# Attention and feed-forward in one kernel: half-swapped q and k weights issued by ScalarE, a swapped copy of x next on SP's queue, one copy of an up product on VectorE

## The chip, the cores and the metric

The kernel runs on one core of a Trainium2 chip. The metric is the time of one execution on the device, in microseconds (us); it is taken several times, and the median is compared. The times of trace rows below come from one profiled execution, counted from its first instruction. The engines are TensorE (PE for matmuls, PEld for weight loads), VectorE (DVE), ScalarE (ACT), GpSimd (POOL) and SyncE (SP); an engine's name with a q behind it (SPq, ACTq) means its queue of issued DMAs.

## What is computed

A transformer block with attention and feed-forward side by side, on 2048 rows of 448 numbers, bfloat16:

```python
xn = layernorm(x)
return x + A(xn, wqkv, wo) + B(xn, w_gate, w_up, w_down)

# A: 16 heads of 28, a row sees itself and the 255 rows before it
q, k, v = split(xn @ wqkv)
p = softmax(where(0 <= i - j < 256, q @ k.T * 28 ** -0.5, -1e9))
A = (p @ v) @ wo
# B: the hidden size is 1792
B = (gelu(xn @ w_gate) * (xn @ w_up)) @ w_down
```

## The kernel before

The 2048 rows are worked in four blocks of 512 (`qb`), the rows of a block in four tiles of 128. The contraction length 448 is three chunks of 128 and a remainder of 64, or seven chunks of 64. The code makes use of the seven chunks: a matmul over 64 rows takes half of TensorE's array, and two such matmuls, one on the upper and one on the lower 64 partitions, run side by side for two different products ("a pair"). For that, each half needs every chunk of normalised, transposed x (`xnT`) on its own 64 partitions. `xsw` is the copy of `xnT` with the two halves of partitions exchanged, and `swap` (L377) makes it by DMA, from SBUF to SBUF, in two pieces, one for each half. The weights for q and k get the same treatment: `wsq` holds half of `wqp` and half of `wkp`, exchanged, and `swap_weights` (L385) makes it by two DMAs of 192 KB. The pair for value tiles (`v_pair`, matmuls at L319) reads `xnT`, `xsw`, `wv`, `wvs`; the pair for q and k of four heads (`qk_pair`, L333) reads `xnT`, `xsw`, `wqp`, `wkp`, `wsq`.

The order of work is written out by hand: each engine works through its instructions in the order of the program. A block consists of attention in nine or ten steps (`steps_of`, `attention`) and then the gates of the feed-forward (`gated`). A step is: scores on TensorE (L600) into a PSUM tile of which attention has one buffer (`score_pool(1)`), an exp on ScalarE over all of it (L604), masks (on GpSimd in the first block, L528), and then work that fills TensorE, taken from `plan`. Products of attention weights with values (`pv`, L570) come two steps or more later. Generators hand out filling work in small pieces, and an entry like `(u, 11)` in `plan` takes eleven of them.

In the first block the filling work is, in this order: `gen_qk`, which finishes q and k of the block's own rows; `gen_up` with the pairs p = 1, 2, 3, 0 of the up product (matmuls at L401, two PSUM tiles each); and from the sixth step on `gen_pairs(1, ...)`, which makes values, q and k for the second block: the value pair of tiles 4 and 5, the value pair of tiles 6 and 7, then q and k. The up products are copied from PSUM to `hT` (L418); the second copy of a pair goes to ScalarE if p is in `shared`, else to VectorE. Four PSUM tiles, handed out in the order in which they come free (`take`, `give`), serve all of these.

`ahead3` (L720), called in the third step of the first block, normalises tiles 5, 6, 7 of x on VectorE, transposes each by a DMA on SP's queue (L175), and issues on SP's queue: the swap of tiles 4 and 5, `swap_weights`, the swap of tiles 6 and 7, and then the loads of gate weights, x, up weights, output weights and down weights. `fill_pads(False)` puts pad columns into `wqp` and `wkp` on GpSimd (L283, L285). SP issues in this order, and each issue waits for what its transfer reads. Copies on the hardware queues take their completion semaphores in turn out of eight, so an issue may also wait for the transfer that had the same semaphore before.

Of the kernel before, what the change touches and what calls it, by code (L numbers as in the profile page):

```python
# [17 lines left out]
P = 128  # L18
# [8 lines left out]
def kernel(  # L27
# [11 lines left out]
    nc = tc.nc  # L39
# [98 lines left out]
    wsq = const.tile([P, 3, H, 32], bf16, name="wsq")  # L138
# [13 lines left out]
    def stat(t):  # L152
        st = work.tile([P, nc.vector.BN_STATS_DIM], f32, name="st")
        nc.vector.bn_stats(out=st[:, :], in_=x_sb[:, t, :])  # L154
        nc.vector.bn_aggr(out=mv_all[:, t, :], in_=st[:, :])
# [44 lines left out]
    spare = ["b0", "b1", "b2", "b3"]  # L200
# [37 lines left out]
    def ring(qb):  # L238

        return slice(qb % 2 * QB, (qb % 2 + 1) * QB)  # L240
# [18 lines left out]
    def gen_qk(gs, others):  # L259

        for g in gs:
            pq = take("pq")
            proj(pq, wqp, 0, g)
            yield 650
            pk = take("pk")
            proj(pk, wkp, 0, g)
            yield 650
            if g in others:
                v_half(*others[g])
            qk_halves(0, g, pq, pk)  # L270
            if g in others:
                v_copy(*others[g], nc.vector.tensor_copy)
            qk_copies(0, g, pq, pk)
            yield 360

    def fill_pads(last):


        def put(dst, src, n, lo):

            src = src.rearrange("p (j d) -> p j d", d=Dh)[:, :, lo:]
            if n == 4:
                nc.gpsimd.tensor_copy(out=dst[:, 12:16, Dh:32], in_=src[:, :, 24:28])  # L283
            src = src[:, :, 0:24].rearrange("p j (g i) -> p g j i", i=8)[:, :, :, 0:4]
            nc.gpsimd.tensor_copy(out=dst[:, 0:12, Dh:32].rearrange("p (g j) i -> p g j i", j=4), in_=src)  # L285

        if not last:
            for c in range(3):
                k = wraw[:, c, D + 12 * Dh:2 * D]
                put(wqp[:, c, :, :], k, 4, 0)  # L290
                put(wkp[:, c, :, :], k, 3, 4)
            return
        put(w3p[0:64, :, :], w3k[0:64, :], 4, 0)
        put(w3p[64:128, :, :], w3k[64:128, :], 3, 4)
        nc.gpsimd.memset(w3p[64:128, 12:16, :], 0.0)
# [81 lines left out]
    def swap(qb, t=None, n=4):  # L377

        t0 = P * (4 * qb if t is None else t)
        to = t0 - qb * QB + ring(qb).start  # L380
        for hi in range(2):
            nc.sync.dma_start(out=xsw[64 * hi:64 * hi + 64, :, to:to + n * P],
                              in_=xnT[64 - 64 * hi:P - 64 * hi, 0:3, t0:t0 + n * P])

    def swap_weights():  # L385

        for hi, src in enumerate((wqp, wkp)):
            nc.sync.dma_start(out=wsq[64 * hi:64 * hi + 64], in_=src[64 - 64 * hi:P - 64 * hi, 0:3])

    def xchunk(qb, hi, c, t0, n):  # L390

# [280 lines left out]
    pvs = [take("pv", D)]  # L672
# [47 lines left out]
    def ahead3():  # L720
        for t in (5, 6, 7):
            norm(t)
            dma_transp(t)
        swap(1, 4, 2)
        fill_pads(False)
        swap_weights()
        swap(1, 6, 2)
        load_ffn(wg, B_w_gate, slice(0, 3))
        nc.sync.dma_start(out=x_sb[:, 12:16, :], in_=xv[:, 12:16, :])
        load_ffn(wu, B_w_up, slice(4, 7))  # L730
        load_ffn(wg, B_w_gate, slice(3, 7))
        wo_v = A_wo.rearrange("(g j d) n -> j d g n", g=4, j=4)
        for j in range(4):
            nc.sync.dma_start(out=wo[32 * j:32 * j + Dh, :, :], in_=wo_v[j])
        for k in (0, 7):
            nc.sync.dma_start(out=wd[:, k:k + 7, :], in_=rows(B_w_down, k, 7))

    for qb in range(NB):
        if qb in (1, 3):
            tc.mark_branch_hint_location("general", hint="LikelyTaken",  # L740
                                         engines=[mybir.EngineType.DVE if qb == 1 else mybir.EngineType.PE])
        early = ()
        if qb == 0:
            new_hT(0)
            early = (0, 1, 2, 3)
            u = chain(gen_qk((1, 2, 3), {1: (3, pvs[3]), 2: (2, pvs[2])}), gen_up(0, (1, 2, 3, 0), (2, 3)))
            w = gen_pairs(1, (("v", 0), ("v", 2), ("k", 0), ("k", 1), ("k", 2)))
            plan = [[(u, 2), ahead, (u, 1)], [lambda: v_dense(2, pvs[2]), (u, 2), ahead2, (u, 1)],
                    [lambda: spare.append(spare.pop(1)), (u, 2), ahead3, (u, 4)], [lambda: stat(8), (u, 11)],
                    [lambda: stat(9), (u, 7), lambda: stat(10), (u, 7), lambda: fill_pads(True)], [(w, 7), "sums", "inverse"],  # L750
                    [(w, 11)], [lambda: stat(11), (w, 6), lambda: rstd(8, 4)],
                    [lambda: q_last(1, nc.vector.tensor_copy), (w, 4), "sums", "inverse", (w, 7)]]
        else:
            d = gen_down(qb - 1)
            if qb < 3:
                u = gen_pairs(qb + 1, (("v", 0), ("k", 0), ("v", 2), ("k", 1), ("k", 2)))
                plan = [[(d, 14)], [(d, 11)], [(d, 11)], [(u, 7)], [(d, 18)], ["sums", (u, 7), "inverse"], [(u, 12)],
                        [(u, 9)], [lambda: q_last(qb + 1, nc.vector.tensor_copy), (d, 5), "sums", "inverse"], [(d, 13)]]
                if qb == 1:
                    for i in range(4):  # L760
                        plan[i].insert(0, lambda t=12 + i: stat(t))
                    plan[4].append(lambda: rstd(12, 4))
            else:
                new_hT(3)
                early = (1, 2, 3, 4, 5, 6)
                u = gen_up(3, early)
                plan = [[(d, 14)], [(d, 4), (u, 5)], [(u, 9)], [(u, 7)], [(d, 18)], [(u, 7)], [(d, 13)], [(d, 5), (u, 7)],
                        [(u, 7)], [(d, 18)]]
        if qb in (1, 2):
            swap(qb + 1)  # L770
        score_pool(1)
        rest, after, flush = attention(qb, plan)
        nc.scalar.preload_act_table(ACT.Gelu_apprx_tanh)
        score_pool(2)
        if qb not in hTs:
            new_hT(qb)

        def hook(f):
            after(f)
            if qb < 3 and f == 4:  # L780
                collect(qb + 1)
            if qb < 3 and f == 10:
                deliver(qb + 1)
            t = ({0: 8, 4: 9, 8: 10, 10: 11} if qb == 0 else {4: 12, 6: 13, 8: 14, 10: 15} if qb == 1 else {}).get(f)
            if t is not None:
                norm(t)
                dma_transp(t)

        gated(qb, early, rest, flush, hook)
        if qb < NB - 1:  # L790
            nc.scalar.preload_act_table_set("natural_log_exp_and_others")
# [151 lines left out]
```

## Time and profile before

| | us |
|---|---|
| median of 3 executions | 216.72 |
| the three executions | 218.1, 216.69, 216.72 |
| the profiled execution | 218.75 |
| its span, first to last instruction | 216.9 |
| busy: TensorE, VectorE, ScalarE, GpSimd | 209.9, 159.3, 131.5, 46.9 |
| TensorE busy, first 56 us | 52.7 |
| TensorE busy, the 160.9 us behind | 157.2 |

The granted clock of TensorE is 1.00 in every stretch of the profile. A line of the timeline begins with start and duration in us, then engine, source line, operation, tile written and tiles read, the size, and the number of instructions merged into the line. In brackets stands the idle time of the engine before it and what ended it. Several merged lines of TensorE overlap, because matmuls on the two halves of the array do. A row of the chain of waits has start, duration and what; a row of the view of waits has the waiting engine and line, what it waited for, and total us, times and longest wait.

### The profile page before, as it was taken

The page shows a single profiled execution, that of the slowest core. Times are in us where ns is not written, and L with a number is a line of the kernel's source. Part 1 is how long each engine was busy: PE and PEld are TensorE (multiplying, and loading weights), DVE is VectorE, ACT ScalarE, POOL GpSimd, SP SyncE. Part 2 cuts the span into 40 slices and gives each one's busy share as a digit, 9 for nine tenths or more (in the row PEclk, how much of TensorE's full clock was granted, in tenths as well). Part 3 has the DMA queues.
Part 4 walks back from the last instruction along what each step waited for, and adds up shares of the span by engine and source line. Part 5 has one row for each costly group of instructions (what it writes and reads, how often), then busy time and mean ns, then how long its engine had stood idle before and what let it go on. Part 6 is the DMA issues. An engine that isn't in the chain of part 4 may idle for free.

```text
span 216.9 us, 6348 instructions
## 1 busy us (share of the span) xinstructions
PE 209.9 (97%) x2722; PEld 101.5 (47%) x2722; DVE 159.3 (73%) x354; ACT 131.5 (61%) x123; POOL 46.9 (22%) x78
## 2 busy tenths in 40 slices
PE   7999979999999999999999999999999999999993
PEld 2433433444445444444445545544444444444892
DVE  6899866999666998588547799576359699586621
ACT  3689677663877986613678697423578676466000
POOL 5287656532000202022000012022000020105001
PEclk9999999999999999999999999999999999999999
DMA  6999579993330000102330000200000000000011
GB/s 187 265 248 149 120 195 253 228 298 57 72 97 21 24 3 25 20 5 48 73 94 24 24 0 3 56 11 3 0 5 19 26 3 24 21 3 2 24 34 38
DMA packets 24193, 15.21 MB, mean 70 GB/s; under 512 B 9856, under 2 KB 24032, under 8 KB 24160
## 3 DMA queue, kind: packets, MB, share of 16 engines
q1 hardware_dynamic: 23216, 14.47, 28.6%
q8 instruction: 22, 0.36, 0.7%
q10 hardware_dynamic: 944, 0.29, 0.5%
q14 instruction: 11, 0.09, 0.1%
HBM read 9.03 MB, written 2.18 MB: 52 GB/s over the span
## 4 chain that ended last, share of the span: by engine, by line
PE 90%; DMA 3%; ACT 2%; DVE 2%; issue 1%; SPq 1%; DVEq 0%; ACTq 0%
PE po L359 26%; PE gt L401 20%; PE u L401 13%; PE sc L600 6%; PE ue L401 6%; PE pq L333 6%; PE ov L570 5%; PE pv L319 3%; DMA xsw<-xnT 2%; ACT p_sb L604 2%; PE pq L190 2%; PE pv L190 1%; DMA x_sb<-in_A_x_dram 1%; DVE st L154 1%; PE s L190 1%
## 5 line engine op out<-in xcount | busy, mean ns | idle before, releaser
L604 ACT ACTIVATE p_sb<-sc 128x2048 bf16<-128x2048 f32 x39 | 73.3, 1878 | 20.2 <-PE sc L600 13.9
L441 ACT ACTIVATE p_sb<-gt 128x1024 bf16<-128x1024 f32 x28 | 28.7, 1024 | 39.5 <-PE gt L401 31.7
L537 POOL TENSOR_TENSOR oN<-oc,l 128x512 bf16<-128x512 f32 x16 | 22.6, 1410 | 137.5 <-DVE l L550 137.5
L359 PE MATMUL po<-wd,hT 128*128 128x448 bf16 (+1 forms) x266 | 47.9, 324 | 0.0
L401 PE MATMUL gt<-xnT,wg 64*128 64x512 bf16 x224 | 45.4, 376 | 0.0
L401 PE MATMUL gt<-xsw,wg 64*128 64x512 bf16 x168 | 40.6, 376 | 0.0
L449 DVE TENSOR_TENSOR hT<-p_sb,u 128x512 bf16<-128x512 bf16 x36 | 23.3, 680 | 19.6 <-PE u L401 11.9
L518 DVE TENSOR_TENSOR p_sb<-p_sb,masks 128x256 bf16<-128x256 bf16 (+1 forms) x90 | 30.2, 390 | 5.0 <-ACT p_sb L604 5.0
L359 PEld LDWEIGHTS <-hT 128*128 128x128 bf16 x266 | 24.6, 98 | 16.0 <-issue 1.4
L401 PE MATMUL u<-xnT,wu 64*128 64x512 bf16 x144 | 29.9, 376 | 0.0
L401 PEld LDWEIGHTS <-wg 64*128 64x128 bf16 x392 | 19.3, 94 | 22.2 <-issue 0.2
L401 PEld LDWEIGHTS <-wu 64*128 64x128 bf16 x392 | 18.6, 94 | 23.2 <-issue 3.1
L401 PE MATMUL u<-xsw,wu 64*128 64x512 bf16 x108 | 26.1, 376 | 0.0
L367 DVE TENSOR_TENSOR res<-po,x_sb 128x448 bf16<-128x448 f32 (+1 forms) x17 | 10.1, 593 | 17.3 <-PE po L359 17.3
L401 PE MATMUL ue<-xnT,wu 64*128 64x512 bf16 x80 | 16.7, 377 | 0.0
L600 PE MATMUL sc<-qT,kT 28*64 28x320 bf16 (+7 forms) x648 | 16.4, 261 | 0.1
L528 POOL TENSOR_SCALAR_AFFINE_SELECT p_sb<-p_sb 128x512 bf16<-128x512 bf16 (+1 forms) x21 | 14.2, 703 | 8.3 <-ACT p_sb L604 8.3
L359 PE MATMUL po<-wo,oN 128*128 128x448 bf16 (+1 forms) x76 | 15.1, 323 | 0.0
L401 PE MATMUL ue<-xsw,wu 64*128 64x512 bf16 x60 | 14.9, 377 | 0.0
L600 PEld LDWEIGHTS <-kT 28*64 28x64 bf16 (+1 forms) x648 | 7.6, 102 | 12.6 <-issue 11.0
L418 DVE CAST hT<-ue 128x512 bf16<-128x512 f32 x18 | 11.5, 680 | 1.0 <-PE ue L401 0.9
L570 PE MATMUL ov<-p_sb,v_sb 64*32 64x320 bf16 (+7 forms) x648 | 11.7, 256 | 0.1
(103 smaller groups left out, 267.0 us busy)
## 6 DMA issues: line engine op xcount, KB each, us to landing
out_dram<-res SPq DMA_DIRECT2D x15, 112.0 KB
wd<-in_B_w_down_dram SPq DMA_DIRECT2D x2, 784.0 KB
x_sb<-in_A_x_dram SPq DMA_DIRECT2D x3, 448.0 KB
wu<-in_B_w_up_dram SPq DMA_DIRECT2D x4, 336.0 KB
xsw<-xnT SPq DMA_DIRECT2D x6, 192.0 KB
wg<-in_B_w_gate_dram SPq DMA_DIRECT2D x2, 448.0 KB
wg<-in_B_w_gate_dram SPq DMA_DIRECT2D x2, 336.0 KB
wraw<-in_A_wqkv_dram SPq DMA_DIRECT2D x2, 252.0 KB
```

The lines of the kernel that those rows point to most:

```text
L333: nc.tensor.matmul(ps, lhsT=w.rearrange("p h d -> p (h d)"), rhs=xchunk(qb, hi, c, qb * QB, QB), start=c == 0, stop=c == 6, tile_position= ...
L359: nc.tensor.matmul(po[:, a:b], lhsT=x[:, k, cs], rhs=wt[:, k, lo + a:lo + b], start=(n == a == 0), stop=(n == len(terms) - 1), skip_group_ ...
L401: nc.tensor.matmul(ps, lhsT=w[64 * hi:64 * hi + 64, c, p * P:(p + 1) * P], rhs=xchunk(qb, hi, c, qb * QB, QB), start=c == 0, stop=c == 6, ...
L418: copy(out=hTs[qb][:, p + 7 * i, :], in_=us[i])
L441: nc.scalar.activation(out=ges[p][:, :, :], in_=gt[:, :, :], func=ACT.Gelu_apprx_tanh)
L449: nc.vector.tensor_tensor(out=hT[:, p + 7 * i, :], in0=ge[:, i, :], in1=u, op=ALU.mult)
L518: nc.vector.tensor_tensor(out=reg, in0=reg, in1=m, op=ALU.mult)
L528: nc.gpsimd.affine_select(out=reg, in_=reg, pattern=mid + [[1 if diag else -1, min(w, P)]], compare_op=ALU.is_ge, fill=0.0, base=0 if diag ...
L537: nc.gpsimd.tensor_tensor(out=oN[:, g, :], in0=oc[:, :], in1=inv, op=ALU.mult)
L570: nc.tensor.matmul(ov[half or 0][32 * j:32 * j + 32, q0:q0 + nq], lhsT=v_sb[r, kt, 4 * g + j, :], rhs=p_sb[r, j, col:col + nq], start=n == ...
L600: nc.tensor.matmul(ss[k0:k0 + nk, j, col:col + nq], lhsT=kT[r, g, kt * P + k0:kt * P + k0 + nk], rhs=qT[r, g, ring(qb).start + q0:ring(qb) ...
L604: nc.scalar.activation(out=p_sb[:, :, 0:ncol], in_=ss[:, :, 0:ncol], func=ACT.Exp, scale=SCALE)
```

## The change

Three edits, all in the first block. The two DMAs of `swap_weights` are issued by ScalarE and not by SP; the call moves out of `ahead3` (third step) to the fourth step's plan, so that they stand behind the fourth step's exp in ScalarE's order. In `ahead3` the swap of tiles 6 and 7 comes straight behind the swap of tiles 4 and 5. Of the four up pairs, only p = 3 leaves its second copy to ScalarE; the second copy of p = 2, which stood between the fourth and the fifth exp on ScalarE, goes to VectorE. Data, sizes and the number of DMAs and matmuls stay.

```diff
     def swap_weights():
 
         for hi, src in enumerate((wqp, wkp)):
-            nc.sync.dma_start(out=wsq[64 * hi:64 * hi + 64], in_=src[64 - 64 * hi:P - 64 * hi, 0:3])
+            nc.scalar.dma_start(out=wsq[64 * hi:64 * hi + 64], in_=src[64 - 64 * hi:P - 64 * hi, 0:3])
...
             norm(t)
             dma_transp(t)
         swap(1, 4, 2)
+        swap(1, 6, 2)
         fill_pads(False)
-        swap_weights()
-        swap(1, 6, 2)
         load_ffn(wg, B_w_gate, slice(0, 3))
...
-            u = chain(gen_qk((1, 2, 3), {1: (3, pvs[3]), 2: (2, pvs[2])}), gen_up(0, (1, 2, 3, 0), (2, 3)))
+            u = chain(gen_qk((1, 2, 3), {1: (3, pvs[3]), 2: (2, pvs[2])}), gen_up(0, (1, 2, 3, 0), (3,)))
...
-                    [lambda: spare.append(spare.pop(1)), (u, 2), ahead3, (u, 4)], [lambda: stat(8), (u, 11)],
+                    [lambda: spare.append(spare.pop(1)), (u, 2), ahead3, (u, 4)], [swap_weights, lambda: stat(8), (u, 11)],
```

## The prediction

> **What bounds the kernel now.** First the head of the page and the chain of work that ended last.
>
> ```profile
> span 216.9 us, 6348 instructions
> PE 209.9 (97%) x2722; PEld 101.5 (47%) x2722; DVE 159.3 (73%) x354; ACT 131.5 (61%) x123; POOL 46.9 (22%) x78
> PE 90%; DMA 3%; ACT 2%; DVE 2%; issue 1%; SPq 1%; DVEq 0%; ACTq 0%
> ```
>
> TensorE is busy for 209.9 of 216.9 us, so an edit off TensorE can win back little more than the 7.0 us in which it does nothing, and part of those are the start and the tail. The view of waits for TensorE alone names only two:
>
> ```profile
> PE pv L319 <- DMA xsw<-xnT: 1.5, 1, 1.5
> PE wps L149 <- DVE wo L123: 1.4, 1, 1.4
> ```
>
> The second is the start, before any data, and the change doesn't touch it. The first is a stall inside the kernel that ends with the landing of a half-swapped copy of x. The chain of waits around it, as start, duration and what, shows how it comes about:
>
> ```profile
> 23.73 1.89 ACT p_sb L604
> 25.67 0.54 SPq L388
> 26.32 0.62 SPq L382
> 26.98 4.36 DMA xsw<-xnT
> 31.39 1.50 PE pv L319 x13
> ```
>
> SP issues the half-swapped weights (L388), then the second half of swapped x (L382, at 26.32 and 26.98). The last piece of x takes 4.36 us from issue to landing at 31.34, and TensorE goes on at 31.39. TensorE's own rows, in the timeline:
>
> ```profile
> 23.61 0.39 PE L401 MATMUL ue<-xnT,wu 64*128 64x512 bf16 x1
> 26.74 0.40 PE L600 MATMUL sc<-qT,kT 28*128 28x128 bf16 x8
> 27.07 0.55 PE L319 MATMUL pv<-wvs,xsw 64*128 64x448 bf16 x2
> 27.27 0.54 PE L319 MATMUL pv<-wv,xnT 64*128 64x448 bf16 x2
> 29.51 0.36 PE L319 MATMUL pv<-wv,xnT 64*128 64x448 bf16 x1
> 31.39 0.36 PE L319 MATMUL pv<-wvs,xsw 64*128 64x448 bf16 x2 [1.52 <-DMA xsw<-xnT]
> 31.59 0.35 PE L319 MATMUL pv<-wv,xnT 64*128 64x448 bf16 x2
> 33.68 0.40 PE L600 MATMUL sc<-qT,kT 28*128 28x384 bf16 x8
> 36.22 0.40 PE L600 MATMUL sc<-qT,kT 28*128 28x384 bf16 x8
> ```
>
> The first pair of value tiles begins at 27.07, on both halves of the array at once, and reaches its second round at 27.27. The second pair begins at 29.51 with one half alone and reaches that round at 31.59. The stall costs (31.59 - 29.51) - (27.27 - 27.07) = 1.88 us, of which 1.52 are idle and the rest is a matmul that ran without its partner. That is the most that the change can take from this trace, 0.9% of the time.
>
> **Part 1: the weights leave SP's queue, so x is issued earlier.** SP's queue:
>
> ```profile
> 18.94 3.28 SPq L175 DMA_TRANSPOSE xnT<-xn  x2
> 22.32 1.22 SPq L175 DMA_TRANSPOSE xnT<-xn  x1
> 23.63 1.28 SPq L382 DMA_DIRECT2D xsw<-xnT  x2
> 25.01 0.56 SPq L388 DMA_DIRECT2D wsq<-wqp  x1
> 25.67 0.54 SPq L388 DMA_DIRECT2D wsq<-wkp  x1
> 27.65 2.60 SPq L81 DMA_DIRECT2D wg<-in_B_w_gate_dram  x2
> ```
>
> Without the two L388 the second half of x is issued at 25.01 and 25.67 in place of 26.32 and 26.98, 1.31 us earlier. It reads what the second and third transposes write. The third is issued by 22.32 + 1.22 = 23.54; its landing isn't printed, only that it was over by 26.32. I take it as over at 25.0, because the copies at 23.63, which read the first transpose of this group, followed the queue without a gap.
>
> When does the half land? The slow end is the 4.36 us of the row: 25.67 + 4.36 = 30.03, which leaves part of the stall, a gain of 31.34 - 30.03 = 1.31. The fast end comes from the first half: its second piece was issued at about 24.27 (half of 1.28 after 23.63) and TensorE read it at 27.07 without a wait, so it took at most 2.80 us. At this price the second half lands by 28.47, 1.04 us before 29.51, and the whole 1.88 is gained. What lies between the two prices is visible in the DMA view of 28 to 30 us:
>
> ```profile
> q8 instruction: 1, 0.02, 4.5%
> ```
>
> One instruction fetch took 4.5% of 16 engines in 2 us, that is one engine for 1.44 us, while the last pieces of x were under way; 4.36 - 2.80 = 1.56 is about that hold. Pieces issued at 25.67 are through before 28, so I take a gain near the fast end, 1.8.
>
> A rule of the Trainium skill speaks for the slow end. DMA: Bandwidth & Descriptors, section "Issuing engines are not separate DMA queues": DMAs started by ScalarE and by SP run on the same engines and interleave, so a second issuing engine saves only the time to issue. By it the sum would be 1.31. No row of before has bulk data from both queues at once, so this trace doesn't decide it.
>
> The loads behind (first gate weights at 27.65, and on to the down weights) move 1.3 us forward too. The view of waits shows no wait of TensorE for any of them; with TensorE 1.8 us earlier their margin shrinks by 0.5 at most. Cost 0.
>
> **Part 2: ScalarE issues the weights.** ScalarE, POOL, and the first issues of the kernel:
>
> ```profile
> 20.31 1.88 ACT L604 ACTIVATE p_sb<-sc 128x2048 bf16<-128x2048 f32 x1 [0.20 <-PE sc L600]
> 22.81 0.59 ACT L418 CAST hT<-ue 128x512 bf16<-128x512 f32 x1 [0.62 <-PE ue L401]
> 29.70 1.88 ACT L604 ACTIVATE p_sb<-sc 128x2048 bf16<-128x2048 f32 x1
> 34.21 1.88 ACT L604 ACTIVATE p_sb<-sc 128x2048 bf16<-128x2048 f32 x1 [0.94 <-PE sc L600]
> 22.11 0.23 POOL L285 COPY wkp<-wraw 128x48 bf16<-128x48 bf16 x1
> 0.81 0.40 SPq L84 DMA_DIRECT2D x_sb<-in_A_x_dram  x1
> 0.82 0.40 ACTq L85 DMA_DIRECT2D x_sb<-in_A_x_dram  x1
> 1.25 1.05 ACTq L88 DMA_DIRECT2D wraw<-in_A_wqkv_dram  x2
> ```
>
> The fourth step's exp (20.31) ends at 22.19, and the copy at 22.81 goes. In its place stand two issues of some 0.55 us (SP's rows; ScalarE's own at 1.25 give 0.53). They wait for POOL's pad copies, done at 22.11 + 0.23 = 22.34. They also wait for transposes, because the program hands out its DMA semaphores in turn: in the built program the first issue waits for the first transpose of the three, the second for the second. That one is issued by 18.94 + 3.28 = 22.22; by the price above it lands by 22.22 + 2.80 = 25.0, and not before 22.3. I take 23.5, half way. ScalarE is then free at 23.5 + 0.6 = 24.1, with ends of 23.5 (the two issues straight after 22.34) and 25.6.
>
> Behind the issues is queued the fifth step's exp, at 23.73 until now (in the chain above). The sixth step's scores, at 26.74, need it finished, since there is one score buffer. So an exp that starts by 26.74 - 1.88 = 24.86 is hidden. At 24.1 it is 0.4 us late and has 0.76 to spare: cost 0. At 25.6 it would cost 0.74; below nothing there is no end, as it wasn't late before. The weights themselves, issued by 24.1, are first used at 32.54 - 1.8 = 30.74 and land by 28.5 even at 4.36 us: cost 0.
>
> ```profile
> 32.54 0.10 PEld L333 LDWEIGHTS <-wsq 64*128 64x128 bf16 x2
> ```
>
> They now travel beside the first half of x, not behind it. That half is read at 27.07 and its landing isn't printed, so its cover may be small. Pushed to the 4.36 us it would land at 24.27 + 4.36 = 28.63 and cost 1.56. I take 0: the weights are issued up to 1.5 us ahead of that half's last piece, and the fetch that made the 4.36 comes later.
>
> **Part 3: one copy on VectorE in place of ScalarE.**
>
> ```profile
> 21.63 1.85 DVE L418 CAST hT<-ue 128x512 bf16<-128x512 f32 x3
> 23.40 0.69 DVE L580 COPY oc<-ov 128x512 f32<-128x512 f32 x1
> 24.01 0.62 DVE L154 BATCH_NORM_STATS2 st<-x_sb 128x6 f32<-128x448 bf16 x1
> 25.33 0.69 DVE L418 CAST hT<-ue 128x512 bf16<-128x512 f32 x1 [0.49 <-PE ue L401]
> ```
>
> A fourth copy costs 24.01 - 23.40 = 0.61 us of pace. The rows at 23.40 and 24.01 slip by that, and the idle 0.49 us before 25.33 takes up all but 0.12. The accumulators that come free later (24.1 by the new copy, 24.7 by the slipped one) are next taken by the last up pair. That pair and the one before it fill TensorE from 23.61 to 26.74, so it starts near 25.2: cost 0, and at most 0.61 without that cover.
>
> **The sum.** -1.8 + 0 + 0 + 0. What is late next: the seventh exp ends at 29.70 + 1.88 = 31.58, and the eighth step's scores come at 33.68 - 1.8 = 31.9. The eighth exp, 34.21 - 1.8 = 32.4, ends at 34.3, and the ninth step's scores come at 36.22 - 1.8 = 34.4. Both just fit, and from there on TensorE runs on as before. The profiled execution took 218.75 us, 1.85 more than its span and 2.03 more than the median of 216.72. It becomes 216.95, its span 215.1, and the median 216.72 - 1.8 = 214.9.
>
> **The rivals.** *Most executions haven't got the stall.* The three times are 216.69, 216.72 and 218.1, 1.4 us apart, about the size of the stall, and the profiled one lies above all. If the collision with the fetch is what makes the slow ones, the median stays at 216.7. Against it: the fetch belongs to the program's own instructions, which are the same in every execution, and even a clean landing (26.98 + 2.80 = 29.78) may come after 29.51. Beside it stands the case that the weights push the first half of x and the stall moves to 27.07: 216.72 - 1.8 + 1.56 = 216.5. Together 0.22.
>
> *ScalarE is held at its issues, and the kernel gets slower.* If descriptors are made for one queue at a time, ScalarE waits while SP, which issues without a break from 18.94 on, has work. Served behind the four copies of x (to 25.67 + 0.64 = 26.3), its two issues end at 27.4. The fifth exp then starts 27.4 - 24.86 = 2.5 too late, and so do the sixth step's scores: 216.72 - 1.8 + 2.5 = 217.4. Served behind the two gate loads as well (to 27.65 + 2.60 - 1.31 = 28.94), the exp starts at 30.0, 5.2 too late: 220.1. It costs from 24.86 on and decides, by eating the gain, from 24.86 + 1.8 = 26.66 on. Against it: at 0.81 and 0.82 SP and ScalarE issue side by side, each in 0.40 us. 0.14.
>
> A rule of the Trainium skill says just this, Perfetto Trace Analysis, section "DMA Instruction — HWDGE (DVE, Sync)": the descriptor generator is shared and locked for exclusive use, and the profiled time of an issue contains the wait for the lock. The two 0.40 us side by side don't bear that out; no row tests it against transposes.
>
> *The change does less than it says.* The third transpose lands only at 26.3, x goes out as before, and only its transfer gets shorter, by 0 to 1.56: 215.2 to 216.7, inside the cases above. 0.04.
>
> **How the numbers follow.** Forecast 0.60, the others as given. One per cent, 2.17 us, is about what a measurement of this kernel can tell from no change. Faster by more than that needs more than the 1.88 of the stall, so the forecast plus 0.3 us of scatter: 0.15. Slower by more needs a fifth exp that starts after 24.86 + 1.8 + 2.17 = 28.83, the far part of the third case: 0.09. Within: 0.76. The range begins 0.3 of scatter below the full stall, 216.72 - 1.88 - 0.3 = 214.5, and reaches over the forecast and the no-gain case to the near end of the slower one, 217.4; outside are its far part and some scatter.
>
> **What would show it.** Right: no wait of TensorE on xsw, the second value pair on both halves at 29.5, ScalarE's issues over by 24.9, later rows of TensorE 1.3 to 1.9 us earlier. Wrong: idle TensorE before the scores at 26.74 (ScalarE held) or before 27.07 (first half late), a landing of x after 29.51 in spite of the earlier issue, or a profile that is 1.8 us shorter beside an unchanged median (the first rival).

## The result, and the profile after

| kernel | median, us | lowest to highest | executions |
|---|---|---|---|
| before | 217.97 | 216.59 to 220.45 | 22 |
| after | 216.88 | 216.48 to 217.59 | 22 |

The ratio after to before is 0.997, 95% interval 0.9955 to 0.9984: a gain between 0.35 and 1.0 us, which is no change by the prediction's bound of one per cent. It compares the means of the executions within 1.5% of a kernel's fastest, which leaves two of before out; the medians lie 1.08 us apart. The forecast was 214.9 us, so 2.0 us too low; the time lies inside the range of 214.5 to 217.4. The 22 times of before fall into groups: six from 216.59 to 216.84, one at 217.31, thirteen from 217.76 to 218.37, two above 220. Two of the three times that the prediction had, and with them its median of 216.72, were from the lowest group. The times of after form one group, and its lowest (216.48) is hardly below before's (216.59).

The profiled execution of after took 216.48 us. Head of its page, with the chain's shares by engine:

```profile
span 214.6 us, 6346 instructions
PE 208.7 (97%) x2722; PEld 101.1 (47%) x2722; DVE 159.8 (74%) x355; ACT 130.7 (61%) x122; POOL 46.4 (22%) x78
PE 94%; DVE 2%; ACT 1%; DMA 1%; issue 1%; DVEq 0%; ACTq 0%
```

The span is 2.3 us shorter than in the profile of before, 0.3 of it ahead of the sixth scores; the share of DMA in the chain falls from 3% to 1%. Its view of waits for TensorE:

```profile
PE wps L149 <- DVE wo L123: 1.4, 1, 1.4
PE tp L183 <- DVE xn L169: 0.4, 2, 0.2
PE pv L190 <- ACT xnT L186: 0.2, 1, 0.2
```

No wait for `xsw` is left; the 1.4 us of the start are as before, and the two others lie ahead of the steps in question. The chain of waits runs through TensorE where it ran through SP and the copy of x:

```profile
23.39 3.13 PE ue L401 x28
26.85 1.45 PE pv L319 x14
29.23 1.43 PE pv L319 x14
```

TensorE's timeline through the sixth to ninth step:

```profile
26.46 0.40 PE L600 MATMUL sc<-qT,kT 28*128 28x128 bf16 x8
28.83 0.40 PE L600 MATMUL sc<-qT,kT 28*128 28x384 bf16 x8
29.17 0.55 PE L319 MATMUL pv<-wvs,xsw 64*128 64x448 bf16 x2
29.37 0.54 PE L319 MATMUL pv<-wv,xnT 64*128 64x448 bf16 x2
31.46 0.40 PE L600 MATMUL sc<-qT,kT 28*128 28x384 bf16 x8
33.99 0.40 PE L600 MATMUL sc<-qT,kT 28*128 28x384 bf16 x8
```

The second value pair reads `xsw` at 29.17 and reaches its second round 0.20 us later, with both halves of the array. From the seventh scores (28.83) to the eighth (31.46) it now takes 2.63 us, where it took 33.68 - 29.18 = 4.50 in the profile of before, whose seventh scores are this row:

```profile
29.18 0.40 PE L600 MATMUL sc<-qT,kT 28*128 28x384 bf16 x8
```

This stage and the one ahead of it (sixth to seventh scores, here 28.83 - 26.46 = 2.37) turn out to be the only places where the profiles of before and after differ by more than the scatter at the start and at the end. SP's queue and ScalarE:

```profile
18.65 4.21 SPq L175 DMA_TRANSPOSE xnT<-xn  x3
22.95 3.90 SPq L382 DMA_DIRECT2D xsw<-xnT  x4
26.90 1.29 SPq L81 DMA_DIRECT2D wg<-in_B_w_gate_dram  x2
```

```profile
22.20 0.52 ACTq L388 DMA_DIRECT2D wsq<-wqp  x1
22.89 0.48 ACTq L388 DMA_DIRECT2D wsq<-wkp  x1
23.45 1.88 ACT L604 ACTIVATE p_sb<-sc 128x2048 bf16<-128x2048 f32 x1 [1.54 <-PE sc L600]
29.44 1.88 ACT L604 ACTIVATE p_sb<-sc 128x2048 bf16<-128x2048 f32 x1
31.97 1.88 ACT L604 ACTIVATE p_sb<-sc 128x2048 bf16<-128x2048 f32 x1 [0.22 <-PE sc L600]
```

The four copies of x now follow each other on SP, over 3.90 us. Four issues at the 0.64 of before make 2.6; the rest is a wait of about 1 us for the third transpose, which lands at 25.55, and a longer first issue, which the last section comes back to. ScalarE issues the weights between the fourth and the fifth exp, and the fifth starts at 23.45, well ahead of the 24.86 up to which it is hidden. VectorE with the fourth copy, 0.6 us longer than the three of before, and with no idle time ahead of it:

```profile
21.35 2.45 DVE L418 CAST hT<-ue 128x512 bf16<-128x512 f32 x4
```

### The profile page after: what moved, and what is told of

The parts are those of the page before. It is cut to its first block, busy times and chain, and to the rows that moved or that the text cites. A ratio compares the mean times of both kernels' runs of the same rounds, so it can differ in the third digit from the quotient of the medians.

```text
span 214.6 us, 6346 instructions
## 1 busy us (share of the span) xinstructions
PE 208.7 (97%) x2722; PEld 101.1 (47%) x2722; DVE 159.8 (74%) x355; ACT 130.7 (61%) x122; POOL 46.4 (22%) x78
## 4 chain that ended last, share of the span: by engine, by line
PE 94%; DVE 2%; ACT 1%; DMA 1%; issue 1%; DVEq 0%; ACTq 0%
PE po L359 26%; PE gt L401 20%; PE u L401 13%; PE ue L401 7%; PE sc L600 6%; PE pq L333 6%; PE ov L570 5%; PE pv L319 4%; PE pq L190 2%; PE pv L190 1%; DMA x_sb<-in_A_x_dram 1%; ACT p_sb L604 1%; DVE st L154 1%; PE s L190 1%; PE pk L190 1%
## 5 line engine op out<-in xcount | busy, mean ns | idle before, releaser
L600 PE MATMUL sc<-qT,kT 28*64 28x320 bf16 (+7 forms) x648 | 16.4, 261 | 0.1
L600 PEld LDWEIGHTS <-kT 28*64 28x64 bf16 (+1 forms) x648 | 7.5, 102 | 12.6 <-issue 11.0
L418 DVE CAST hT<-ue 128x512 bf16<-128x512 f32 x19 | 12.1, 679 | 0.5 <-PE ue L401 0.4
```

The costliest lines, as they stand in the source:

```text
L418: copy(out=hTs[qb][:, p + 7 * i, :], in_=us[i])
L600: nc.tensor.matmul(ss[k0:k0 + nk, j, col:col + nq], lhsT=kT[r, g, kt * P + k0:kt * P + k0 + nk], rhs=qT[r, g, ring(qb).start + q0:ring(qb) ...
```

## The experiments

In the expectations, theory A says that the stall of before comes and goes from one execution to the next, so that a median can belong to executions with or without it; theory D says that the first half of x, now beside the weights, gives part of the gain back. Other letters stand for the rivals that an expectation sets against these. Stages are told by the starts of the scores (L600) in TensorE's timeline: "six to seven" is the first value pair, "seven to eight" the second.

### The kernel before, again: does the stall come in every execution?

Nothing is edited. One set of 12 executions with one profile, then three more profiles on another chip.

> The kernel before, unchanged, against itself. Theory A (the stall before the second value pair comes and goes from execution to execution, since it hangs on one landing): the times fall in two groups about 1.3 us apart, one near 216.7 and one near 218.0, ratio 1.000 within 0.3%; a profile of about 218 us shows an idle of TensorE of 1 to 1.6 us before L319, one of about 216.7 us shows less than 0.4. Theory B (the stall is there in every execution, and the change gives back about 1 us in most of its own): an idle of about 1.5 us before L319 whatever the time of the profiled execution, and the two groups come from another place.

> The kernel before, one more profile. Theory A (the stall comes and goes): time and stall go together. With the stall taken as the start of the eighth step's scores less the start of the seventh's, over the 2.63 us that it takes without a wait, the time is 215.1 + 1.2 + stall within 0.3: near 217.6 with a stall of 1.2 to 1.5, near 216.3 with none, 218.5 with 1.9. The last piece of swapped x lands before 29 in the one case and after 30 in the other. Theory B: a stall of 1.4 or more in each.

> As for the profile before it: by theory A stall 0 to 0.2 with a time near 216.3 (about one in five), else 1.2 to 1.9 with 217.5 to 218.5; by theory B 1.4 or more always.

> As for the two before it: by theory A stall 0 to 0.2 with a time near 216.3 (about one in five), else 1.2 to 1.9 with 217.5 to 218.5; by theory B 1.4 or more always.

| profiled execution of the kernel before | its time, us | seven to eight, us | stall over 2.63, us |
|---|---|---|---|
| the one of the prediction | 218.75 | 4.50 | 1.87 |
| again | 217.55 | 4.00 | 1.37 |
| again_2 | 217.61 | 3.92 | 1.29 |
| again_3 | 217.81 | 4.09 | 1.46 |
| again_4 | 216.58 | 2.62 | 0 |

All other stages agree within 0.03 us, apart from the start and the end, each up to 0.3 us longer or shorter. An execution takes 216.2 to 216.9 us and its stall beside. The set of 12 ran at a median of 217.66 against 217.83 for the same kernel beside it (ratio 1.0002, 0.9989 to 1.0015), none of the 30 times below 217.4: on that chip the lowest group didn't turn up at all. Over all 92 executions of before that were timed beside some other kernel, 16 lie below 216.9.

SP's rows of "again", where TensorE waits 1.02 us for x:

```profile
18.66 4.59 SPq L175 DMA_TRANSPOSE xnT<-xn  x3
26.02 1.28 SPq L382 DMA_DIRECT2D xsw<-xnT  x2
```

SP's rows of "again_4", and those of TensorE in its second value pair, from the timeline:

```profile
18.75 3.87 SPq L175 DMA_TRANSPOSE xnT<-xn  x3
25.39 1.28 SPq L382 DMA_DIRECT2D xsw<-xnT  x2
29.32 0.55 PE L319 MATMUL pv<-wvs,xsw 64*128 64x448 bf16 x2
29.52 0.53 PE L319 MATMUL pv<-wv,xnT 64*128 64x448 bf16 x2
```

The three transposes went out in 3.87 us in place of 4.59, so the second half of x was issued 0.63 us earlier, and TensorE read it at 29.32 without a wait. By the trace's records of landings its last piece was there at 28.38; in "again" 15 of the 16 pieces were there by 29.02, and the last came at 30.57. The DMA view of 28 to 30 us shows the instruction fetch in "again_4" too:

```profile
q8 instruction: 1, 0.02, 3.1%
```

That is 1.0 us on one engine. So the fetch is there in an execution without a stall as well, and an issue 0.6 us earlier is enough to be past it. The trace's packets tell when the fetch runs. In the four profiles with a stall it begins 1.16 to 1.40 us after the last copy of x is issued, and the last piece of that copy lands 1.51 to 1.57 us after the fetch ends; in "again_4" it begins 2.05 us after the issue, and no piece is late. Theory A is shown. That the fetch makes the piece late rests on these times; no run moved the fetch alone.

An earlier fetch of 16 KB goes with the pace of the transposes. In four of all seventeen profiles of this document it begins between 17.95 and 18.44 us, "again_4" among them, and the three transposes go out in 3.83 to 3.87 us; in the other thirteen it begins between 19.36 and 20.20, and they take 4.21 to 4.91. Why it comes sooner in some executions isn't shown.

### x later still: is it the landing of x that sets the end?

```diff
-        swap(1, 6, 2)
         load_ffn(wg, B_w_gate, slice(0, 3))
+        swap(1, 6, 2)
```

In the kernel before, the second half of x goes behind the first two loads of gate weights.

> The kernel before with the first two gate loads (672 KB) ahead of the second half of x on SP's queue, so that the half is issued 1.3 to 2.6 us later and stands behind these loads at the DMA engines. The stall must be there in every execution: idle before L319 of 3.5 to 6 us, time 2 to 4.5 us above the stalled executions of before. Theory A: the two groups of times close up to one group, as the landing no longer falls on either side of the need, and the median is 219.5 to 222.5. Theory B: same shift, the scatter stays as it was.

223.42 us, ratio 1.0243 (1.0212 to 1.0274). The idle time is inside the expectation, the time is not: it rose by 5.6 us. The chain's row for x and TensorE's row behind the stall:

```profile
27.85 6.32 DMA xsw<-xnT
```

```profile
34.22 0.56 PE L319 MATMUL pv<-wvs,xsw 64*128 64x448 bf16 x2 [4.68 <-DMA xsw<-xnT]
```

The view by stretches (stretch, length, then busy time of PE, PEld, DVE, ACT, POOL with the number of instructions, granted clock, DMA share, GB/s):

```profile
31.00:32.00 1.00, 0.00 (x0) 0.00 (x0) 0.08 (x1) 0.26 (x1) 0.67 (x2) 0.91 1.17 257
32.00:33.00 1.00, 0.00 (x0) 0.00 (x0) 0.00 (x0) 0.00 (x0) 1.00 (x2) 0.50 1.11 325
...
38.00:39.00 1.00, 1.00 (x13) 0.14 (x12) 0.39 (x2) 0.00 (x0) 0.00 (x0) 0.68 1.14 236
```

The granted clock falls to 0.50 while TensorE waits and is back at 1.00 only at 38.64 (0.68 over the stretch from 38 is 0.64 us at a half and the rest at one). From 34.22 to 38.64, TensorE does half of the work, a loss of 2.2 us. With the 4.68 of idle that is 6.9; seven to eight takes 9.80 us, 7.2 more than without a stall. The landing of x does set the end, and a stall of this length costs half as much again by the clock. The six times aren't the one group that theory A expected: two are 222.03 and 222.07, four lie from 223.40 to 223.90, and why isn't shown. The stalls of before, up to 1.52 us of idle, leave the clock at 1.00.

### The order alone, all on SP's queue

```diff
         swap(1, 4, 2)
+        swap(1, 6, 2)
         fill_pads(False)
         swap_weights()
-        swap(1, 6, 2)
```

Against the kernel before; ScalarE issues nothing and keeps its copy.

> Only the order on SP's queue is changed: second half of x, then the weights, all from SP. The second half is issued 1.3 us earlier as in the change; the weights then land behind it, issued at 26.3 and 26.98, first needed at about 30.7. If ScalarE's queue isn't needed (the order is what counts), the time is that of the change, ratio 0.995 to 0.998. If the fetch now hits the weights as it hit x, they land at 31.3 and the wait moves to L333: idle of 0.5 us there, ratio 0.997 to 1.000. Theory A expects no second group 1.3 us higher, theory B the same scatter as in the kernel before.

217.09 us, ratio 0.996 (0.9946 to 0.9975). The wait for x is gone, and two others stand in its place, as the view of waits for weight loads shows:

```profile
PEld L401 <- DMA wg<-in_B_w_gate_dram: 0.6, 1, 0.6
PEld L333 <- DMA wsq<-wkp: 0.5, 1, 0.5
```

The chain of waits now runs through the gate weights:

```profile
32.23 11.75 DMA wg<-in_B_w_gate_dram
...
44.03 3.19 PE gt L401 x27
```

Weight loads wait 0.5 us for the half-swapped k weights, which are last in line, and 0.6 us for the last gate weights. Here the k weights have the late piece: 15 of 16 land by 29.60, the last at 31.10, 1.65 us after the fetch ends. Seven to eight took 3.03 us in this profile in place of 2.63, and the time from the first gate matmul to the next block 16.37 in place of 15.9. SP's four copies of x, with no weights beside them, go out without a gap in 2.63 us (from 23.31), where the change took 3.90. Six to seven is 2.43 us here, as in the kernel before.

### The change without the copy on VectorE

```diff
-            u = chain(gen_qk((1, 2, 3), {1: (3, pvs[3]), 2: (2, pvs[2])}), gen_up(0, (1, 2, 3, 0), (3,)))
+            u = chain(gen_qk((1, 2, 3), {1: (3, pvs[3]), 2: (2, pvs[2])}), gen_up(0, (1, 2, 3, 0), (2, 3)))
```

> The change without its third part: ScalarE issues the weights and still makes the second copy of the pair p = 2 behind them. ScalarE is then free for the fifth exp about 0.6 us later, at about 24.0 in place of 23.45, under the 24.86 at which it starts to cost. Both theories as predicted: same time as the change (within 0.1%), ratio 0.995 to 0.998. If the copy's bank is late for TensorE, up to 0.6 us more.

216.53 us, ratio 0.9945 (0.9931 to 0.9959). The view of waits has none of TensorE for x or for an exp. But one half of the array begins the first value pair at 26.80 and the other at 27.10, behind the landing of the first half of x at 27.05, and six to seven takes 2.67 us: 0.23 more than in the kernel before. The copy on VectorE brings nothing and costs nothing that can be told: the change itself measured 216.63 and 216.71 in the sets below, and the intervals overlap.

### The change again: is anything given back?

Nothing is edited: two sets of timed executions with a profile each, and one profile alone.

> The changed kernel, unchanged, on the chip of the other kernels of this set. Theory C (the gain is cut short by the gate weights: in the profile after, the last piece of the load for gates 3 to 6 landed at 42.87, 0.05 us before its use at 42.92, while before it had 2.4 us to spare): where the profiled execution takes over 217.0 us, TensorE waits 0.2 to 1 us for wg within L401; one near 216.5 has no wait. Theory A (only the stall of the kernel before comes and goes; nothing new is late in the change): no such wait in any execution, times above 217 come from the start of the kernel. Ratio 0.994 to 0.998 by both.

> The changed kernel, one more profile. No wait on swapped x by either theory: 2.6 to 2.7 us from the seventh step's scores to the eighth's. Theory C: gates 3 to 6 get their weights within 0.3 us of the need, on one side or the other; a time over 217.0 shows a wait on wg of the excess over 216.5.

> The changed kernel once more, on the chip of the next two. Theory D (ScalarE's weights run ahead of and beside the first half of swapped x, so that TensorE waits for that half in some executions, 0 to 0.7 us, from the sixth step's scores to the seventh's): 2.37 to 3.10 us from the one to the other, the time 216.4 plus what it is over 2.44; last piece of the first half landed at 26.8 to 27.7. Theory C (the gate weights are late): a wait within L401 in the executions over 217.

| profiled execution of the change | its time, us | six to seven, us | seven to eight, us |
|---|---|---|---|
| after, shown above | 216.48 | 2.37 | 2.63 |
| change_again | 216.50 | 2.45 | 2.63 |
| change_3 | 216.98 | 3.10 | 2.62 |
| change_4 | 216.69 | 2.82 | 2.62 |

The sets gave 216.63 us, ratio 0.9959 (0.9943 to 0.9974), and 216.71, ratio 0.9957 (0.9934 to 0.9981). The stall of the second pair came in none of the four, but the first pair, 2.43 or 2.44 in every profile of before, now varies, and in "change_3" there is a wait for swapped x that neither theory of its expectation had. In "change_3" the chain shows the copy, and the timeline what waited:

```profile
24.78 2.85 DMA xsw<-xnT
```

```profile
26.94 0.36 PE L319 MATMUL pv<-wv,xnT 64*128 64x448 bf16 x1
27.68 0.36 PE L319 MATMUL pv<-wvs,xsw 64*128 64x448 bf16 x2 [0.38 <-DMA xsw<-xnT]
```

The first half of x landed at 27.63; one half of the array began at 26.94 alone, and the other followed 0.74 us later. The cost is 3.10 - 2.44 = 0.66 us. In "change_4" the same piece took 2.89 us, and 0.38 were lost; in "again" it took 2.2 (issued at 24.01, landed at 26.21). This is theory D, between nothing and 0.7 us; over the four profiles its mean is 2.69 - 2.44 = 0.25. The kernels compared here bear it out: the piece takes 2.77 to 2.89 us in all seven profiles in which ScalarE's weights go out beside it, and 2.20 or 2.21 in the ten others.

The weights also slow what is ahead of x. The third transpose, which the second half of x waits for, takes 3.89 to 3.95 us from issue to landing in those seven profiles and 2.49 to 2.52 in the ten others. So the change gives back part of the 1.31 us that SP's shorter queue gains, and in some executions all of it. In "change_3" the second half of x went out at 26.47 and 27.11, later than in any profile of the kernel before, and still took 2.20 us and landed at 29.30. There the fetch began 1.82 us after the last issue, as it does in all seven (1.77 to 1.85). The stall is gone because the last copy of x is clear of the fetch, and not because it always goes out earlier; what sets the time of the fetch no run shows.

### The loads behind x: what margin have the gate weights?

```diff
         load_ffn(wg, B_w_gate, slice(0, 3))
-        nc.sync.dma_start(out=x_sb[:, 12:16, :], in_=xv[:, 12:16, :])
         load_ffn(wu, B_w_up, slice(4, 7))
         load_ffn(wg, B_w_gate, slice(3, 7))
+        nc.sync.dma_start(out=x_sb[:, 12:16, :], in_=xv[:, 12:16, :])
```

This puts the last rows of x behind the gate weights, so that these land about 1.8 us sooner. It was made in the change, in the kernel before, and in the kernel with the order alone.

> The change with one load moved: the last four tiles of x (448 KB, needed only in the second block) are issued behind the gate weights and not ahead of them. Theory C: at some 250 GB/s the gate weights land 1.8 us earlier, near 41.1, the wait is gone in all executions, and the median falls to the change's fastest times, 216.2 to 216.5, ratio 0.992 to 0.995, with a scatter under 0.5 us. Theory A: same as the change, ratio and scatter.

> The kernel before with the same load of x moved behind the gate weights. Its gate weights landed 2.4 us before their use and its stall ends on swapped x, issued ahead of all these loads. Both theories: no gain, ratio 0.998 to 1.002. If it gains over 0.3%, the loads were in the way of the kernel before too, and theory C is too narrow.

> No DMA from ScalarE: on SP's queue the first half of x, the second half, the weights, two gate loads, up weights, gate weights for gates 3 to 6, and only then the last tiles of x. Theory D: first half landed by 26.4 in every execution and 2.44 us from the sixth step's scores to the seventh's; the weights take the hit of the fetch and cost 0 to 0.5 us in L333; the gate weights, 448 KB earlier, cost nothing, where the same order without that cost 0.45. Median 216.4 to 216.7, at or below the change's. If ScalarE's queue is what makes the gain, it stays at 217.0 or more.

The opposite, in the change: the output weights, which are needed much later, go ahead of the last gate weights.

```diff
-        load_ffn(wg, B_w_gate, slice(3, 7))
...
             nc.sync.dma_start(out=wo[32 * j:32 * j + Dh, :, :], in_=wo_v[j])
+        load_ffn(wg, B_w_gate, slice(3, 7))
```

> The change with the load of the output weights (392 KB) issued ahead of the gate weights for gates 3 to 6. Theory C: these land some 1.6 us later and TensorE waits for all of it: 1.2 to 2 us above the change, 217.9 to 218.9, wait on wg within L401 of that size in the profile. Theory A: the load has room, at most 0.3 us above the change.

| kernel | median, us | ratio to before, 95% | first gate matmul to next block, us |
|---|---|---|---|
| change, x load last | 216.51 | 0.9956, 0.9929 to 0.9983 | 15.9 |
| before, x load last | 217.74 | 1.0001, 0.9978 to 1.0024 | 15.9 |
| order alone, x load last | 216.90 | 0.9963, 0.9941 to 0.9986 | 15.9 |
| change, gates later | 218.06 | 1.0026, 1.0001 to 1.0051 | 17.08 |

In the waits of "change, gates later", for weight loads and for matmuls, the cover is gone:

```profile
PEld L401 <- DMA wg<-in_B_w_gate_dram: 1.3, 1, 1.3
PE gt L401 <- DMA wg<-in_B_w_gate_dram: 0.8, 1, 0.8
```

That kernel loses the gain. In the change itself no such wait shows, but in the profile of after its last gate weights land at 42.87 and are read at 42.92; in that of before, they landed at 42.71 and were read at 45.15. The cover fell from 2.44 us to 0.05. These are the two ends: it is 0.23 to 0.82 in the other profiles of the change, and 0.80 to 1.31 in the other four of the kernel before. Giving it back with the x load last makes no difference that can be told from the change beside it (216.63, ratio 0.9959), so the thin cover holds in most executions. In the kernel before it makes none either; the profile of that kernel, at 216.29 us, happened to be one without the stall, and among its other times are 218.21 and 220.12.

The third row compares issuers: with the order alone and the gate weights secured, ScalarE's part is replaced by a reordering on SP, and 216.90, above the 216.4 to 216.7 that were expected, stands against 216.71 for the change in the same set, with overlapping intervals. The order, with x ahead of the weights, is what brings the gain; which engine issues the weights can't be told apart by the time.

### The weights behind the fifth exp

```diff
-            u = chain(gen_qk((1, 2, 3), {1: (3, pvs[3]), 2: (2, pvs[2])}), gen_up(0, (1, 2, 3, 0), (3,)))
+            u = chain(gen_qk((1, 2, 3), {1: (3, pvs[3]), 2: (2, pvs[2])}), gen_up(0, (1, 2, 3, 0), ()))
...
-                    [lambda: spare.append(spare.pop(1)), (u, 2), ahead3, (u, 4)], [swap_weights, lambda: stat(8), (u, 11)],
-                    [lambda: stat(9), (u, 7), lambda: stat(10), (u, 7), lambda: fill_pads(True)], [(w, 7), "sums", "inverse"],
+                    [lambda: spare.append(spare.pop(1)), (u, 2), ahead3, (u, 4)], [lambda: stat(8), (u, 11)],
+                    [swap_weights, lambda: stat(9), (u, 7), lambda: stat(10), (u, 7), lambda: fill_pads(True)], [(w, 7), "sums", "inverse"],
```

One step later, the weights would no longer travel beside the first half of x. The copy of p = 3 goes to VectorE too.

> The change with ScalarE's two issues one step later, behind the fifth exp, and no up copy left on ScalarE. In the built program the two issues then wait for the landing of the first pieces of both halves of x, so the second can't start before about 26.9, and the sixth exp stands behind it. Theory D: the first half is undisturbed, landed by 26.4, 2.44 us there; ScalarE is held instead, the sixth exp starts at 27.4 in place of 26.9, and TensorE waits up to 0.5 us for its score buffer at the seventh step's scores. Median 216.6 to 217.2. By the opposite view (the weights don't disturb the first half) it is the change plus 0.5: 217.1 to 217.5.

222.40 us, ratio 1.0202 (1.0168 to 1.0236): a miss by more than 5 us. The rows of ScalarE, and of TensorE behind its two waits, from the timeline:

```profile
26.01 0.52 ACTq L388 DMA_DIRECT2D wsq<-wqp  x1
27.32 0.47 ACTq L388 DMA_DIRECT2D wsq<-wkp  x1
27.84 1.88 ACT L604 ACTIVATE p_sb<-sc 128x2048 bf16<-128x2048 f32 x1 [2.29 <-POOL w3p L295]
29.77 0.40 PE L600 MATMUL sc<-qT,kT 28*128 28x384 bf16 x8 [0.66 <-ACT p_sb L604]
35.48 0.61 PE L333 MATMUL pk<-xsw,wsq 64*128 64x512 bf16 x1 [3.67 <-DMA wsq<-wkp]
```

The two issues don't run one behind the other: the second waits until 27.32, the sixth exp behind it starts at 27.84, and the seventh scores come 0.66 us late. That is the prediction's second rival at a small price. Six to seven takes 3.09 us, which is 2.43 without these 0.66: the first half is undisturbed, as theory D has it. The large price is the transfer, in the chain of waits:

```profile
27.32 8.12 DMA wsq<-wkp
```

The first two gate loads are out ahead of the k weights by then, the 16 engines are full from 30 us on, and the weights take 8.12 us and land at 35.43. TensorE stands still for 3.67 us, and the clock goes to a half again, until 41.54, as these stretches show:

```profile
34.00:35.00 1.00, 0.00 (x0) 0.00 (x0) 0.00 (x0) 0.00 (x0) 1.00 (x1) 0.86 1.11 227
...
41.00:42.00 1.00, 1.00 (x21) 0.19 (x10) 0.21 (x1) 0.00 (x0) 0.20 (x1) 0.73 0.99 213
```

0.66 + 3.67 + (41.54 - 35.48) / 2 = 7.4 us, and the span, 222.2, is 7.3 above that of "change_4" beside it. What held the second issue is the third copy of x, whose semaphore it reuses in the built program: by the trace ScalarE's wait for that semaphore is over at 27.26, and the copy landed at 27.24. The first issue shows the same with the first copy, 25.96 and 25.94. The code doesn't make it wait for the `w3p` that the view names.

## Why the prediction was wrong in size

**What bounds the kernel, and the stall's removal: right in kind.** The stall before the second value pair was the thing to win, taking the weights out of its way wins it, and no profile of the change has it. The two exps named as late next just fit, as forecast: 29.44 + 1.88 = 31.32 ahead of 31.46, and 31.97 + 1.88 = 33.85 ahead of 33.99.

**The sum: the step that failed.** "It becomes 216.95, its span 215.1, and the median 216.72 - 1.8 = 214.9." The profiled time came out 0.5 us better than the first part of that sentence. The last part takes the stall of one execution off a median of others. The runs show that 216.72 is the time of an execution with no stall: 216.58 in "again_4", 216.29 in the profile with the x load last. The stall is 1.29 to 1.46 us in three of five profiles, 1.87 in the one on hand, and nothing in one; so the kernel's usual time was near 217.8, and removing the stall gave about 216.8 and not 214.9. The gain of 1.8 was also too large: a usual stall of 1.29 to 1.46, less the 0.25 that the first half of x gives back, is 1.0 to 1.2, and the medians differ by 1.08. The working held the sign of it, 2.03 us between the profiled execution and the median, beside a stall of 1.88.

**The first rival, given too little.** It named this mechanism, with 216.7 as the median, and was set back because the fetch is in every execution. The fetch is, but x is not always in flight when it comes: 0.63 us of earlier issue in "again_4" was enough. It was wrong in proportion too, since most executions do have the stall.

**Part 1.** The second half of x was to go out at 25.01 and 25.67. In the profile of after it went out at 25.60 and 26.25, because the third transpose landed at 25.55 and not by 25.0; it is 0.7 us earlier than before and not 1.31. The reading of before was right, where that transpose landed at 24.81; what the working left out is that the weights slow the transpose, by 1.4 us. In "change_3" it landed at 26.41, and x went out no earlier than before: the third rival, which was given 0.04, and yet with the whole stall gone. The landing at 28.44, where 28.47 was forecast, is luck: the issue was 0.6 us later and the transfer 0.6 shorter than in the working. The gain was at the fast end for the reason given, as none of its pieces was late, with the fetch at 28.03. The rule of the Trainium skill, DMA: Bandwidth & Descriptors, section "Issuing engines are not separate DMA queues", would have left 0.57 us of the stall, and none was seen. The part of it that the engines are shared agrees with the k weights that took 8.12 us behind SP's gate loads, although ScalarE issued them, and with the slower transpose. The sentence that no row of before has data from both queues at once overlooks the start, where both engines issue loads from 0.81 to 2.3 us.

**The first half beside the weights: mis-sized.** It was taken at 0 and priced at 1.56 at worst. It measures 0 to 0.66, and 0.25 in the mean of four profiles. The reason for the 0, that the weights are issued first, didn't hold: the first half's last piece took 2.77 to 2.89 us beside them and 2.20 without.

**The loads behind: right in cost, wrong in reason.** They were to move 1.3 us forward with 0.5 of cover lost at most. From 30 us on the engines are full, in after as in the two kernels with a long wait; its view by stretches, with the DMA share as the last number but one:

```profile
30.00:32.00 2.00, 2.00 (x26) 0.75 (x24) 1.93 (x5) 1.78 (x3) 1.21 (x4) 1.00 1.10 220
...
40.00:42.00 2.00, 2.00 (x20) 0.88 (x18) 1.93 (x4) 0.82 (x2) 0.46 (x2) 1.00 1.12 232
```

The last gate weights were issued 1.0 us earlier (31.97 for 32.97), and 15 of their 16 pieces landed 0.96 earlier (41.65 for 42.61), but the last one 0.16 later (42.87 for 42.71), while TensorE came to them 2.2 us sooner. In after the last piece of each load from the rows of x on is 1.1 to 1.2 us behind the other 15, in before about 0.1; why isn't shown.

**Part 2.** Right: in the change the fifth exp started at 23.45, 23.57, 24.27 and 23.78, where 24.1 was estimated and 24.86 was the limit. The rival by which ScalarE waits behind SP's whole queue didn't come true here. **Part 3.** Right: no wait on VectorE's copies, and the same time without them.

## What to carry to other kernels

Before taking a stall off a median, see whether the profiled execution is one of those that the median stands for: where the times fall into groups as far apart as a stall is long, that stall is probably there in one group and not in the other, and the change moves one group onto the other. A transfer issued earlier on full DMA engines need not land earlier, so look at what is queued behind for the cover it loses. A copy that is moved to another engine's queue travels beside what it used to follow: see what that slows. When a small copy is moved to another queue, count which large loads will then be ahead of it.

## What was not expected of the hardware

**One issue is longer beside another engine's, others aren't.** The prediction doubted a lock on the descriptor generator. SP's first copy of x in the profile of after, beside ScalarE's second issue (22.89, 0.48 us):

```profile
22.95 0.96 SPq L382 DMA_DIRECT2D xsw<-xnT  x1
```

The same copy with the weights behind the fifth exp, and no issue of ScalarE beside it:

```profile
23.70 0.62 SPq L382 DMA_DIRECT2D xsw<-xnT  x1
```

In the profile of after SP's issue and ScalarE's overlap by 0.42 us (22.95 to 23.37), and SP's takes 0.34 longer than alone; in "change_again" the overlap is 0.41 and the issue takes 0.95. This alone would agree with the Trainium skill, Perfetto Trace Analysis, section "DMA Instruction — HWDGE (DVE, Sync)", that the generator is locked and an issue's profiled time contains the wait. Other overlaps don't: with the weights behind the fifth exp, ScalarE's issues at 26.01 and 27.32 overlap SP's at 25.73 and 27.05 by 0.32 and 0.38 us. SP's two take 0.60 and 0.65, and the same two without ScalarE beside them, in the order alone, 0.60 and 0.64; ScalarE's take 0.52 and 0.47, no more than SP's own issues of these weights (0.54 to 0.56). In after, ScalarE's first issue lies wholly within SP's third transpose (21.64 to 22.86), and takes 0.52 too. So a lock isn't shown, and what lengthens the one issue stays open. Its cost is a third of a microsecond each time, far from the 2.5 us of the rival.

**The clock after a wait.** In the two kernels with a long wait the granted clock fell to a half 2.3 us (31.82 - 29.54) and 2.9 us (34.72 - 31.81) after TensorE's last work, and was full again 4.4 us (38.64 - 34.22) and 6.1 us (41.54 - 35.48) after work resumed. By the trace's records of the clock, both stretches at a half last 6.83 us, and both begin 27.31 us after the first record (4.51 and 7.40): two and eight times 3.41 us. The Trainium skill, TensorE: Matmul & The Clock Gate, section "Part 1: The HAM clock gate", gives half rate after an idle window and full rate after a busy one, each of about 3.4 us and not tied to when work stops or starts. The half rate agrees, and so do the steps of 3.41 us and the rises, each at the end of the first step that is all work (35.23 to 38.65 and 38.13 to 41.54). The falls came at the end of a step that wasn't all idle, with 1.1 and 0.5 us of work at its start.

**One piece late.** The instruction fetch holds one of 16 DMA engines for 1.0 to 1.4 us, and a copy spread over all 16 waits for its one late piece: in the prediction's profile 15 of 16 pieces by 29.29, the last at 31.34, 1.51 us after the fetch ended. What decides for the last copy of x, in the kernel before and in the change, is how far ahead of the fetch it is issued: its piece is late at 1.16 to 1.40 us, and not at 1.77 to 2.05.

Open: what sets the times of the two fetches, and the 7 of 92 times of before between 219 and 220.5 us, of which no profile was taken.
